# Loading a gate matrix and two expert matrices through GpSimd's DMA queue instead of ScalarE's

## The chip, the cores and the metric

The kernel runs on one core of one Trainium2 chip. The metric is the device time of one launch, in microseconds (us). A core has five engines that work from instruction queues of their own: TensorE (PE in the profile, with its weight loads shown apart as PEld), VectorE (DVE), ScalarE (ACT), GpSimd (POOL) and SyncE (SP). Sixteen DMA engines move data between the chip's main memory and the core's SBUF. A DMA is issued by an instruction in the queue of SP, ACT or Pool, and its landing is a semaphore that reaches 16.

## The reference, cut to what matters

Two stages are fused. The first is a linear recurrence along the sequence, for 8 batches of 6400 steps with 128 channels. The second treats all 51200 results as rows `x` of a mixture of low-rank adapters with 8 experts of rank 16, of which the two with the largest gate logits are used.

```
h = a[:, t] * h + b[:, t];  x[:, t] = h                 # 8 x 6400 x 128, float32
logits = x @ w_gate                                     # w_gate: 128 x 8
w = softmax over the two largest logits of a row
out = x + sum over the two experts e of  w_e * ((x @ A[e]) @ B[e])   # A: 8 x 128 x 16, B: 8 x 16 x 128
```

## The kernel before

The 51200 rows are cut into 100 units of 512 rows. A unit `w` goes through these steps, whose names are used below:

- `lda`, `ldb`: SP loads `a` and `b` (L632). Most loads bring two units (512 KB); four bring one (256 KB). The ring in SBUF holds 8 such loads of each, and a load waits until the unit that used its place 8 loads earlier has been transposed.
- `A`, `AB`: PE transposes `a` and `b` into PSUM with the identity `ident_f` (L632 to L677, recorded at L98). `aev`: ACT copies the transposed `a` to SBUF (L686). `scan`: DVE runs the recurrence (L710).
- `ZL`: PE multiplies the scanned block by `cst_h[:, 0:136]`, which holds the gate weights beside all of A (L749, recorded at L94). `zl`: ACT copies the result out (L767).
- gating (L781 to L907): DVE, Pool and ACT find the two largest logits and make the weights, for groups of one to three units.
- `mul`, `T`, `tev`, `D`, `oev`: weights times `x @ A` (Pool or DVE, L926), PE transposes, ACT or DVE copies back (L942), PE adds `x` and the product with B (L962, recorded at L94), ACT copies the sum to `outt` (L978). `st`: SP stores it, two units at a time, in an order that holds each store back by some 20 units (L995).

Every step is an operation of a planner (`_Plan`, L101). Each has a cost, a due key, a list of engines and a list of operations that it needs. `schedule` simulates all engines with one DMA link, starting at 700 ns, and always takes the operation that could start first, and of several that start together the one with the lowest key; a constant's key is its small negative number alone, so -110 goes ahead of -108. The order that comes out is written into each engine's queue, and the chip then works each queue strictly in that order with semaphore waits. A change of an operation's engine or number can so change the order of everything behind it.

The constants are set up at the head. Pool clears `ident_f` (`id0`, L435) and puts ones on its diagonal (`id`, L442). DVE makes `high`, `pick`, `mine` and the 16-bit copy `idh` from it (L490 to L524, L577). Three DMAs bring the weights to the tile `cst_f`: `wg_in` the gate weights (4 KB, 32 bytes for each of 128 partitions), `A_in` and `B_in` the expert arrays (64 KB each, 512 bytes a partition). Behind them:

- `spr0` on Pool and `spr1` on DVE (L533) spread A by expert, as soon as `A_in` and `mine` are done; `selA` (L542, eight matmuls on PE) gathers it, and `cstA` (L560, ACT) writes it to `cst_h`.
- `cstg` and `cstB` (L588, both on Pool) cast the gate weights and B to 16 bits, after `wg_in` and `B_in`.
- The first `ZL` needs `cstg` and `cstA`; the first `D` needs `cstB`.
- `table` (L480) is an activation on ACT that loads its table early.

All DMAs are recorded at L429, in `add_dma`.

Of the kernel before, what the change touches and what calls it, by code (L numbers as in the profile page):

```python
# [100 lines left out]
class _Plan:  # L101
# [15 lines left out]
    def add(self, name, eng, kind, unit, busy, emit, deps=(), dma=None, mode=None, takes=(), gives=None):  # L117
        self.ops[name] = _Op(name, eng, kind, unit, busy, self.latency, emit, list(deps), dma, mode, takes, gives)
# [161 lines left out]
def bass_associative_scan_2x2__then__mixture_of_adapters_kernel(  # L280
# [9 lines left out]
    E = moe_w_gate.shape[1]  # L290
# [78 lines left out]
    with ExitStack() as stack:  # L369
# [4 lines left out]
        cst_f = sb(nc.sbuf_tensor("cst_f", [128, E + 256], F32))  # L374
# [45 lines left out]
        def add_dma(name, eng, unit, starts, slot, ns, deps=(), kind="dma", issue=450.0, after=2000.0):  # L420

            if slot not in dma_sem:
                dma_sem[slot] = [sb(nc.semaphore("q_" + "_".join(map(str, slot)))), 0]
            dma_sem[slot][1] += 16 * len(starts)
            sem, value = dma_sem[slot]

            def emit(h):
                for dst, src in starts:
                    last = h.dma_start(dst, src).then_inc(sem, 16)  # L429
                return last  # L430

            add(name, eng, kind, unit, issue * len(starts), emit, deps, (sem, value, ns, after))
# [18 lines left out]
            ["id0"],  # L451
        )

        add_dma("wg_in", "act", -110, [(cst_f[:, 0:E], moe_w_gate[:, :])], ("wg",), 80.0, (), "fix", 450.0, 2000.0)
        add_dma(
            "A_in",
            "act",
            -109,
            [(cst_f[:, E : E + 128], moe_A.rearrange("e (h l) r -> (e h) (l r)", l=8))],
            ("A",),  # L460
# [5 lines left out]
        )  # L466
        add_dma(
            "B_in",
            "act",
            -108,  # L470
            [(cst_f[:, E + 128 : E + 256], moe_B.rearrange("e r d -> (e r) d"))],
            ("B",),
# [617 lines left out]
```

## Time and profile before

| what | value |
|---|---|
| median of 5 runs | 201.36 us (201.22 to 201.92) |
| the profiled execution's own time | 201.92 us |
| its span in the profile | 200.1 us |
| PE, ACT, DVE, POOL busy | 181.2, 179.5, 173.7, 158.4 us |
| moved by DMA | 79.30 MB, 396 GB/s over the span |
| read from main memory, written to it | 52.56 MB, 26.21 MB |
| granted TensorE clock, mean | 0.988 |

The profile page gives busy time by engine, then the span in 40 slices of 5 us with one digit (tenths) for each engine and the rate of all DMAs in GB/s. Section 3 of the page gives each DMA queue: its number, packets, MB, and the time that its packets took as a share of sixteen engines' span. Queue q1 is SP's, q10 is ACT's; q8 and q14 fetch instructions. In a timeline each row has the start, the length, the engine (a trailing q means its sequencer, which issues DMAs), the line, the operation and the tiles; brackets give the idle time ahead of it and what ended that. In a table of windows the DMA column is the mean busy share of the 16 DMA engines, and may pass 1 where packets of two queues overlap.

### The profile page before, as it was taken

How to read it: one execution, taken by the hardware profiler on the slowest of the kernel's cores; microseconds unless marked ns; L12 is line 12 of the kernel's file. 1: busy time of each engine (PE TensorE's matmuls, PEld its weight loads, DVE VectorE, ACT ScalarE, POOL GpSimd, SP SyncE). 2: the span in 40 equal slices, each digit the busy share in tenths (PEclk: the TensorE clock that was granted, in tenths of full speed). 3: DMA queues.
4: the chain of work that ended last, by engine and by line, in shares of the span. 5: the costliest groups of instructions: out<-in, count | busy, mean ns of one | idle time of the engine just before them, and what ended most of it. 6: DMA issues, size and time to landing. Idle time of an engine off the chain costs nothing.

```text
span 200.1 us, 8009 instructions
## 1 busy us (share of the span) xinstructions
PE 181.2 (91%) x3202; PEld 161.5 (81%) x3202; DVE 173.7 (87%) x302; ACT 179.5 (90%) x463; POOL 158.4 (79%) x278
## 2 busy tenths in 40 slices
PE   7687899999999999999999999999999999897640
PEld 4476788899999989899889998889898998795530
DVE  3599899999999998999989898799797998989910
ACT  3487999999999999999999999999999999898740
POOL 2243749989898999988699999998999988888700
PEclk9999999999999999999999999999999999999995
DMA  6999999999999999999999999999999999999991
GB/s 206 374 422 401 409 409 403 409 407 406 406 416 418 414 414 417 414 414 414 416 417 410 416 417 414 414 419 416 414 417 414 411 418 416 411 379 391 415 389 64
DMA packets 22629, 79.30 MB, mean 396 GB/s; under 512 B 2624, under 2 KB 2880, under 8 KB 22592
## 3 DMA queue, kind: packets, MB, share of 16 engines
q1 hardware_dynamic: 22160, 78.65, 97.8%
q8 instruction: 25, 0.41, 0.8%
q10 hardware_dynamic: 432, 0.14, 0.3%
q14 instruction: 12, 0.10, 0.1%
HBM read 52.56 MB, written 26.21 MB: 394 GB/s over the span
## 4 chain that ended last, share of the span: by engine, by line
PE 49%; DVE 15%; ACT 13%; DMA 12%; issue 3%; POOL 2%; SPq 2%; POOLq 1%; DVEq 0%; ACTq 0%
PE ps L94 25%; PE ps L98 24%; DMA a_in<-in_a_dram 12%; DVE xT L710 11%; ACT outt L978 4%; ACT a_st L686 4%; ACT zl L767 3%; DVE zwT L942 2%; SPq L429 2%; POOL zw L926 2%; POOLq L369 1%; ACT pn L816 1%; DVE zw L926 1%; POOL d L880 1%; ACT g L905 0%
## 5 line engine op out<-in xcount | busy, mean ns | idle before, releaser
L710 DVE TENSOR_TENSOR_SCAN xT<-a_st,xT,ps 128x512 f16<-128x512 f32 x96 | 120.2, 1252 | 10.5 <-PE ps L98 4.1
L926 POOL TENSOR_TENSOR zw<-zl,g 128x512 f16<-128x512 f32 x93 | 99.1, 1070 | 8.6 <-ACT g L905 6.5
L767 ACT COPY zl<-ps 128x408 f32<-128x408 f32 (+1 forms) x139 | 73.6, 536 | 0.9 <-PE ps L94 0.9
L98 PE MATMUL ps<-ident_f,a_in 64*128 64x64 f32 (+1 forms) x792 | 68.6, 229 | 2.3 <-DMA a_in<-in_a_dram 2.3
L98 PE MATMUL ps<-ident_f,b_in 64*128 64x64 f32 (+1 forms) x792 | 67.0, 229 | 1.8 <-DVE m L851 1.0
L686 ACT COPY a_st<-ps 128x512 f32<-128x512 f32 x100 | 61.5, 634 | 6.7 <-PE ps L98 6.0
L98 PEld LDWEIGHTS ps<-ident_f,a_in 64*128 64x128 f32 (+1 forms) x792 | 56.9, 139 | 9.7 <-DMA a_in<-in_a_dram 3.2
L978 ACT COPY outt<-ps 128x512 f32<-128x512 f32 x100 | 61.3, 628 | 2.1 <-PE ps L94 1.3
L98 PEld LDWEIGHTS ps<-ident_f,b_in 64*128 64x128 f32 (+1 forms) x792 | 55.9, 139 | 3.0 <-DVE m L851 1.1
L94 PE MATMUL ps<-cst_h,xT 128*128 128x136 f16 x400 | 50.3, 234 | 0.7 <-DVE xT L710 0.5
L94 PE MATMUL ps<-ident_h,xT 128*128 128x128 f16 x400 | 42.4, 229 | 1.4 <-DVE zwT L942 1.0
L98 PE MATMUL ps<-ident_h,zw 128*128 128x128 f16 x400 | 39.1, 220 | 3.7 <-DVE zw L926 2.0
L94 PEld LDWEIGHTS ps<-cst_h,xT 128*128 128x128 f16 x400 | 36.0, 148 | 4.5 <-DVE xT L710 1.3
L94 PE MATMUL ps<-cst_h,zwT 128*128 128x128 f16 x400 | 38.7, 219 | 0.0
L942 DVE COPY zwT<-ps 128x256 f32<-128x256 f32 x89 | 35.6, 408 | 2.6 <-PE ps L98 2.5
L94 PEld LDWEIGHTS ps<-ident_h,xT 128*128 128x128 f16 x400 | 32.9, 147 | 3.4 <-DVE zwT L942 2.3
L98 PEld LDWEIGHTS ps<-ident_h,zw 128*128 128x128 f16 x400 | 24.9, 97 | 7.7 <-DVE zw L926 3.0
L94 PEld LDWEIGHTS ps<-cst_h,zwT 128*128 128x128 f16 x400 | 27.1, 99 | 0.0
L816 ACT ACTIVATE pn<-d 128x96 f32<-128x96 f32 (+2 forms) x72 | 23.1, 329 | 0.8 <-POOL d L858 0.6
L866 POOL TENSOR_TENSOR L<-zl,pn 128x96 f32<-128x96 f32 (+2 forms) x34 | 12.8, 378 | 6.6 <-ACT pn L816 6.3
L888 POOL TENSOR_TENSOR d<-d 128x96 f32<-128x96 f32 (+2 forms) x36 | 13.8, 382 | 3.8 <-DVE d L841 3.3
L895 POOL TENSOR_TENSOR um<-d,pn 128x96 f32<-128x96 f32 (+2 forms) x36 | 14.2, 393 | 2.7 <-ACT pn L816 1.3
(38 smaller groups left out, 86.7 us busy)
## 6 DMA issues: line engine op xcount, KB each, us to landing
a_in<-in_a_dram SPq DMA_DIRECT2D x49, 512.0 KB, 15.5
b_in<-in_b_dram SPq DMA_DIRECT2D x49, 512.0 KB, 15.5
out_dram<-outt SPq DMA_DIRECT2D x49, 512.0 KB, 15.5
a_in<-in_a_dram SPq DMA_DIRECT2D x2, 256.0 KB, 8.9
b_in<-in_b_dram SPq DMA_DIRECT2D x2, 256.0 KB, 4.3
out_dram<-outt SPq DMA_DIRECT2D x2, 256.0 KB, 6.8
cst_f<-in_moe_A_dram ACTq DMA_DIRECT2D x1, 64.0 KB, 3.4
cst_f<-in_moe_B_dram ACTq DMA_DIRECT2D x1, 64.0 KB, 5.3
```

Source lines behind the costliest of these rows:

```text
L94: return self.handle.matmul(*args, **kwargs)
L98: return self.handle.transpose(*args, **kwargs)
L686: lambda h: h.copy(a_st[w % NAS][:, :], bank(("a", w))[:, :]),
L710: last = h.tensor_tensor_scan(out=x_at(lo, hi), data0=a_st[w % NAS][:, lo:hi], data1=bank(("b", w))[:, lo:hi], initial=init, op0=ALU.mult, ...
L767: return h.copy(zl[:, r0 : r0 + n, :], src)
L816: lambda h: h.activation(v(pn[s]), v(src[s]), ACTF.Relu, bias=bias, scale=scale),
L866: lambda h: h.tensor_tensor(out=v(L2[s]), in0=Lg, in1=v(pn[s]), op=ALU.subtract),
L888: lambda h: h.tensor_tensor(out=v(d1[s]), in0=v(d1[s]), in1=v(d2[s]), op=ALU.add),
L895: lambda h: h.tensor_tensor(out=v(um[s]), in0=v(d1[s]), in1=v(pn[s]), op=ALU.subtract),
L926: lambda h: h.tensor_tensor(out=oview, in0=zview, in1=gview, op=ALU.mult),
L942: return copy(zwT[v % NZT][:, :].bitcast(F32), bank(("O", v))[:, 0 : UT // 2])
L978: return copy(outt[:, v % NOUT, :], bank(("O", v))[:, :])
```

## The change

The three loads of the weights are issued by Pool (GpSimd's queue, in which software writes the descriptors) instead of ACT. The gate weights' number goes from -110 to -107, so among the three they come last instead of first. Nothing else is edited: the same bytes go to the same places, and the same operations wait for them.

```diff
-        add_dma("wg_in", "act", -110, [(cst_f[:, 0:E], moe_w_gate[:, :])], ("wg",), 80.0, (), "fix", 450.0, 2000.0)
+        add_dma("wg_in", "pool", -107, [(cst_f[:, 0:E], moe_w_gate[:, :])], ("wg",), 80.0, (), "fix", 450.0, 2000.0)
         add_dma(
             "A_in",
-            "act",
+            "pool",
             -109,
             [(cst_f[:, E : E + 128], moe_A.rearrange("e (h l) r -> (e h) (l r)", l=8))],
             ("A",),
...
         add_dma(
             "B_in",
-            "act",
+            "pool",
             -108,
             [(cst_f[:, E + 128 : E + 256], moe_B.rearrange("e r d -> (e r) d"))],
             ("B",),
```

## The prediction

> **What bounds the kernel now.** I read the page first: the rate of the DMAs by slices of 5 us, and the queues.
>
> ```profile
> GB/s 206 374 422 401 409 409 403 409 407 406 406 416 418 414 414 417 414 414 414 416 417 410 416 417 414 414 419 416 414 417 414 411 418 416 411 379 391 415 389 64
> q1 hardware_dynamic: 22160, 78.65, 97.8%
> q10 hardware_dynamic: 432, 0.14, 0.3%
> ```
>
> From slice 3 on the rate is flat at 400 to 420 GB/s, and SP's queue alone fills 97.8% of sixteen engines' span. ACT's queue, the one that the change empties, fills 0.3%, which is 0.003 x 200.1 = 0.6 us of each DMA engine. Next I read SP's timeline.
>
> ```profile
> 8.48 0.44 SPq L429 DMA_DIRECT2D a_in<-in_a_dram  x1
> 55.77 1.05 SPq L429 DMA_DIRECT2D a_in<-in_a_dram  x1
> 161.80 31.45 SPq L429 DMA_DIRECT2D out_dram<-outt  x19
> ```
>
> An issue takes 0.44 us while there is room and about 1.05 us later, one straight after the other: SP is held by the DMA engines, whose 512 KB take 512 KB / 413 GB/s = 1.27 us. After 161.8 us only 19 stores remain, and compute ends with a copy at 192.2 us. Is that copy the bound? The windows of the last microseconds and the time to landing of the last store (issued at 192.85 us) answer that; beside it stands the first load, of the same 256 KB, which went into empty queues.
>
> ```profile
> 194.00:195.00 1.00, 0.00 (x0) 0.00 (x0) 0.00 (x0) 0.00 (x0) 0.00 (x0) 1.00 1.00 399
> 195.00:196.00 1.00, 0.00 (x0) 0.00 (x0) 0.00 (x0) 0.00 (x0) 0.00 (x0) 0.73 0.59 227
> 197.00:198.00 1.00, 0.00 (x0) 0.00 (x0) 0.00 (x0) 0.00 (x0) 0.00 (x0) 0.50 0.09 37
> 198.00:199.00 1.00, 0.00 (x0) 0.00 (x0) 0.00 (x0) 0.00 (x0) 0.00 (x0) 0.50 0.06 25
> ```
>
> The columns after the stretch are its length, the busy time of PE, PEld, DVE, ACT and POOL, the granted clock, the DMA share and GB/s. Then the two landing times, the last store's first:
>
> ```profile
> DMA to landing us min/median/max: 6.8/6.8/6.8
> DMA to landing us min/median/max: 2.7/2.7/2.7
> ```
>
> The last store lands 6.8 us after its issue where an empty queue needs 2.7. A share of 0.06 is 0.06 x 16 = one DMA engine: the end is the one engine that is still behind while fifteen are done. For the store ahead (issued at 191.54 us, landing also 6.8 us later, with 256 KB in between, 0.6 us) the queue's part is 6.8 - 2.7 - 0.6 = 3.5 us. So compute could end about 3.5 to 4.1 us later and the last byte would still leave at the same time. I call this the cover. The chain of waits shows PE lines instead from 29 us on, because it follows semaphores, not a DMA engine's backlog.
>
> **The change part by part.** The start of the timeline before has every step that moves.
>
> ```profile
> 0.73 0.41 ACTq L429 DMA_DIRECT2D cst_f<-in_moe_w_gate_dram  x1
> 1.17 0.45 ACTq L429 DMA_DIRECT2D cst_f<-in_moe_A_dram  x1
> 1.65 0.45 ACTq L429 DMA_DIRECT2D cst_f<-in_moe_B_dram  x1
> 3.64 0.19 POOL L588 CAST cst_h<-cst_f 128x8 f16<-128x8 f32 x1 [2.18 <-DMA cst_f<-in_moe_w_gate_dram]
> 4.72 1.48 POOL L533 TENSOR_TENSOR spread<-cst_f,mine 128x384 f16<-128x384 f32 x1 [0.90 <-DMA cst_f<-in_moe_A_dram]
> 7.04 0.29 POOL L588 CAST cst_h<-cst_f 128x128 f16<-128x128 f32 x1 [0.84 <-DMA cst_f<-in_moe_B_dram]
> 8.46 0.31 PE L94 MATMUL ps<-cst_h,xT 128*128 128x136 f16 x2
> ```
>
> *ACT.* Three issues of 0.41 + 0.45 + 0.45 = 1.3 us go. ACT's table load then runs earlier, but its next work, the copy at 4.67 us, waits for PE's transposes of the first load. Gain: nothing.
>
> *Pool's order, worked by hand from the planner's rules.* Pool starts with `id0`; at 900 ns `id` is not yet ready, so `A_in` goes, then `id`, `B_in`, `wg_in`. Its planned landings become 5110 (A), 7310 (B) and 7580 (gate) instead of 5880, 7390 and 4470 ns. So `spr0` comes first among the users, then `cstB`, then `cstg`; and `selA`, ready earlier in the plan, probably goes ahead of unit 1's transposes on PE. Pool's queue behind the three issues is `spr0`, which waits for A anyway.
>
> *Price of an issue on Pool.* No row shows one. From below: ACT's 0.45 us. From above: Pool's costliest row here, `spr0`, 1.48 us. I take 1.0, nearer neither, and keep both ends. Then `A_in` is issued from 0.93 to 1.9 us, `id` is done at 2.3, `B_in` ends at 3.3 and `wg_in` at 4.3 us. (Ends: 1.4 and 2.4 for A; 2.6 and 5.7 for the gate.)
>
> *Late constants.* A landed 3.0 us after its issue ended (1.62 to about 4.6): now 4.9 us (4.4 to 5.4), so `spr0` ends at about 6.5 instead of 6.2. The gate weights took 2.4 us when queues were empty; B, issued into full ones, took 7.0 - 2.1 = 4.9. Issued third they resemble B: 4.3 + 4.9 = 9.2 us (from 2.6 + 2.4 = 5.0 to 5.7 + 4.9 = 10.6). With the cast `ZL` starts at about 9.5 instead of 8.46: about 1.0 us late (0 to 2.5). Behind it on PE's queue wait the transposes of later units, then the scans; `D` needs `cstB` only after 13 us. This lateness is covered twice: from 9 to 29 us PE still waits for loads (the chain there is 24 us of DMA of `a_in`), and at the end by the 3.5 us. Ring places come back late too, but loads were landing up to 15.5 us after issue, so the DMA engines have that much queued. On the path: 0. If the cover were gone it would cost its 1.0 us (at most 2.5).
>
> *`ident_f`.* `id` ends at 2.3 instead of 1.46 us; its first user on PE starts at 3.52, on the first load's landing. Cost 0; at 1.48 us an issue `id` is at 2.8, still covered.
>
> *The DMA engines themselves.* This is the only part on the path. The bytes are the same, on the same sixteen engines. Rates in the windows from 2 to 7 us are 250, 370, 343, 334 and 301 GB/s, against 410 after: (2050 - 1598) / 410 = 1.1 us lost while the queues fill and ACT's small packets pass between SP's. Most I can gain is that 1.1 us, if it is all due to the early small packets and they later pass for nothing; most I can lose is another 0.6 us, if the packets of a software queue take twice as long. A shift in time alone gives neither: the packets must still pass through engines that are full. I take 0.
>
> The page *DMA: Bandwidth & Descriptors* of the Trainium skill, section *SWDGE vs HWDGE vs iDMA*, calls hardware descriptor generation the faster setup, and its *Specifications* give about 1 us to the first byte for GpSimd's path against 0.6: by that each load would land some 0.4 us later, an estimate. *SBUF — State Buffer*, section *SBUF: two separate sides*, speaks against the change more strongly: while VectorE runs certain copies, GpSimd cannot write descriptors. No run shows it yet; by that rule the constants could slip by as much as VectorE's early work, and as long as this stays under the cover the sum is unchanged.
>
> *Sum.* Path terms: 0 (ACT) + 0 (lateness, 1.0 under a cover of 3.5) + 0 (DMA, -1.1 to +0.6). The profiled execution is its span of 200.1 and 1.8 around it, 201.92, the highest of five runs; the same change against the median 201.36 gives 201.4 us.
>
> **The rivals.**
>
> *Slower: the lateness outgrows the cover.* One mechanism: constants arrive late, or the new order lets compute's tail slip, until the last copy ends after 192.8 + 3.5 = 196.3 us. It decides when compute is more than 3.5 us late, and each us beyond costs one: 6 us late gives 201.4 + 2.5 = 203.9, 4.5 gives 202.4. For it: PE, ACT and DVE are 98%, 98% and 93% busy from 29 to 178 us (146.26, 146.19, 138.74 of 149), so nothing is made up there, and the planner's order changes from 1 us on. Against: the bounds above reach 2.5.
>
> *Faster: the start is freed.* The first loads no longer share the engines with 432 small packets, and the 1.1 us comes back in part: 200.3 to 200.8. For it: the low rates stand just where q10's packets pass. Against: they must pass at some time, and 0.6 of the 1.1 us is their own time.
>
> *It does nothing at the queue level.* If a Pool issue is as cheap as ACT's, all lands as before and the time is 201.4: the same number as mine.
>
> **How the numbers follow.** A measurement of this kernel can tell about 0.3% (0.6 us) from no change, so the middle is 200.8 to 202.0. My forecast with the last rival: 0.42. Slower: 0.34, for the untested order behind the change and a price of an issue that no row shows. Faster: 0.24. The range from 200.4 to 203.2 takes in most of the faster case and the slower one up to 1.8 us beyond the cover; it leaves out about 0.08 below and 0.12 above. The middle case alone would be 200.9 to 201.9.
>
> **What would show it.** Right: SP's 19 stores still end with a last landing some 6 us after issue; `spr0` ends near 6.5 us and the first `ZL` starts near 9.5; the Pool issues are 1 us apart; windows from 2 to 7 us hold about 1.6 MB. Wrong: the last store lands in about 2.7 us (compute became the bound), or the windows from 2 to 7 us carry much more (the start was freed), or a gap in Pool's rows longer than 1.5 us for an issue.

## The result and the profile after

The changed kernel took 202.5 us (median of 40 runs, 201.25 to 203.74), the kernel before beside it 201.57 us (77 runs). The ratio is 1.0041 with a 95% interval of 1.0032 to 1.0051, so the change costs about 0.0041 x 201.57 = 0.83 us. By the bound that the prediction set itself (0.3%, 0.6 us) that is slower, not the same. The profiled execution took 202.36 us, 0.44 more than the one of before, with a span of 200.6 us.

The page of after first: the rates by slices of 5 us, and the two queues.

```profile
GB/s 185 360 417 408 409 410 403 410 400 411 407 416 414 416 414 416 413 413 419 413 416 410 417 415 416 418 413 417 417 417 413 413 418 413 413 365 316 406 335 213
q1 hardware_dynamic: 22160, 78.65, 97.7%
q0 software_dynamic: 96, 0.14, 0.3%
```

SP's queue still fills its 97.7%: the bound is where it was. The same 0.14 MB now go in 96 packets instead of 432, and take the same share, 0.3%. The first two slices are lower (185 and 360 against 206 and 374), so are the four ahead of the last (365, 316, 406 and 335 against 379, 391, 415 and 389), where stores wait for late compute, and the last holds 213 against 64.

The start of the timeline of after:

```profile
1.30 0.70 POOL L429 DMA_DIRECT2D cst_f<-in_moe_A_dram  x1 [0.36 <-POOL ident_f L435]
2.34 0.56 POOL L429 DMA_DIRECT2D cst_f<-in_moe_B_dram  x1
2.90 0.71 POOL L429 DMA_DIRECT2D cst_f<-in_moe_w_gate_dram  x1
6.23 1.47 POOL L533 TENSOR_TENSOR spread<-cst_f,mine 128x384 f16<-128x384 f32 x1 [2.62 <-DMA cst_f<-in_moe_A_dram]
10.05 0.19 POOL L588 CAST cst_h<-cst_f 128x8 f16<-128x8 f32 x1 [1.26 <-DMA cst_f<-in_moe_w_gate_dram]
10.30 0.42 PE L94 MATMUL ps<-cst_h,xT 128*128 128x136 f16 x2 [0.59 <-POOL cst_h L588]
```

An issue on Pool takes 0.56 to 0.71 us, `id` (0.3 us) stands between the first two, and the last one ends at 3.6 us; on ACT all three had ended by 2.1. A landed at about 6.1, B at 8.4 and the gate weights at 10.0 us; they had landed at 4.6, 7.0 and 3.6. The first `ZL` starts 1.84 us later, at 10.30.

At the other end, the last output copies on ACT, the landing time of the last store, and two windows (columns as in the prediction):

```profile
193.99 1.57 ACT L978 COPY outt<-ps 128x512 f32<-128x512 f32 x3 [0.33 <-PE ps L94]
```

```profile
DMA to landing us min/median/max: 4.5/4.5/4.5
```

```profile
195.00:196.00 1.00, 0.00 (x0) 0.00 (x0) 0.00 (x0) 0.56 (x2) 0.00 (x0) 1.00 0.68 274
198.00:199.00 1.00, 0.00 (x0) 0.00 (x0) 0.00 (x0) 0.00 (x0) 0.00 (x0) 1.00 0.23 88
```

Compute ends at 193.99 + 1.57 = 195.56 us, 2.7 us later than before (192.82). Its last store lands 4.5 us after its issue. With 2.7 us for an empty queue, 1.8 us of that is still backlog: compute has used up part of the cover, not all of it, and yet the end is later. The prediction's two signs were some 6 us (right) and about 2.7 (wrong); 4.5 lies between them.

### The profile page after: what moved, and what is told of

The parts are those of the page before. It is cut to its first block, busy times and chain, and to the rows that moved or that the text cites. A ratio compares the mean times of both kernels' runs of the same rounds, so it can differ in the third digit from the quotient of the medians.

```text
span 200.6 us, 8030 instructions
## 1 busy us (share of the span) xinstructions
PE 183.8 (92%) x3202; PEld 164.2 (82%) x3202; DVE 173.9 (87%) x302; ACT 179.3 (89%) x461; POOL 160.6 (80%) x283
## 3 DMA queue, kind: packets, MB, share of 16 engines
q1 hardware_dynamic: 22160, 78.65, 97.7%
## 4 chain that ended last, share of the span: by engine, by line
PE 46%; DVE 22%; ACT 19%; issue 4%; DMA 4%; POOL 3%; ACTq 0%; DVEq 0%; POOLq 0%
PE ps L98 24%; PE ps L94 22%; DVE xT L710 18%; ACT a_st L686 7%; ACT outt L978 5%; ACT zl L767 4%; DMA cst_f<-in_moe_w_gate_dram 4%; DVE zwT L942 3%; ACT pn L816 2%; POOL zw L926 1%; ACT g L905 1%; ACT zwT L942 1%; POOL cst_f L429 1%; DVE m L851 0%; POOL d L858 0%
## 5 line engine op out<-in xcount | busy, mean ns | idle before, releaser
L767 ACT COPY zl<-ps 128x408 f32<-128x408 f32 (+1 forms) x139 | 71.9, 525 | 1.5 <-PE ps L94 1.5
L686 ACT COPY a_st<-ps 128x512 f32<-128x512 f32 x100 | 60.3, 618 | 6.8 <-PE ps L98 5.4
L978 ACT COPY outt<-ps 128x512 f32<-128x512 f32 x99 | 60.4, 617 | 1.7 <-PE ps L94 1.2
L98 PEld LDWEIGHTS ps<-ident_f,b_in 64*128 64x128 f32 (+1 forms) x792 | 56.7, 141 | 0.4
L94 PE MATMUL ps<-ident_h,xT 128*128 128x128 f16 x400 | 43.0, 231 | 1.0 <-DVE zwT L942 0.6
L942 DVE COPY zwT<-ps 128x256 f32<-128x256 f32 x90 | 36.3, 409 | 3.7 <-PE ps L98 3.7
L816 ACT ACTIVATE pn<-d 128x96 f32<-128x96 f32 (+2 forms) x72 | 21.9, 314 | 0.4 <-POOL d L858 0.3
L895 POOL TENSOR_TENSOR um<-d,pn 128x96 f32<-128x96 f32 (+2 forms) x37 | 13.6, 368 | 4.3 <-ACT pn L816 2.7
```

What stands on the lines that cost most here:

```text
L94: return self.handle.matmul(*args, **kwargs)
L98: return self.handle.transpose(*args, **kwargs)
L686: lambda h: h.copy(a_st[w % NAS][:, :], bank(("a", w))[:, :]),
L767: return h.copy(zl[:, r0 : r0 + n, :], src)
L816: lambda h: h.activation(v(pn[s]), v(src[s]), ACTF.Relu, bias=bias, scale=scale),
L895: lambda h: h.tensor_tensor(out=v(um[s]), in0=v(d1[s]), in1=v(pn[s]), op=ALU.subtract),
```

## The experiments

Four explanations stood against each other; the letters are those of the expectations below. **Order** (theory O): the planner's new order makes the late start of compute count. **Lateness** (L): the constants come late, and compute with them, whatever the order. **Queue** (Q): Pool's software queue holds up the DMA engines. **Time of issue** (T): small packets that are issued when the DMA engines are already full of SP's loads cost time that they do not cost at the very start, whichever engine issues them. "Compute ended" is the end of the last output copy in the profile; it was 192.82 us before.

### Order alone, and queue alone

The first kernel keeps after's order on every engine, but ACT issues the loads, at the head of its queue. Within the planner, behind its simulation:

```diff
+        loads = [ops[n] for n in ("wg_in", "A_in", "B_in")]
+        self.order["pool"] = [op for op in self.order["pool"] if op not in loads]
+        self.order["act"] = loads + self.order["act"]
+        for op in loads:
+            op.eng = "act"
```

> The changed kernel's order in every queue, but the three loads issued by ACT as before. Theory Q (the loads' passage through Pool's queue holds up some DMA engines in the first 10 us, and the last DMA engine sets the end): within 0.3 us of the kernel before, about 201.6. Theory O (the new order and the later start of compute use up the cover at the end): about 202.5, as the changed kernel, and the last store lands under 5 us after its issue.

It took 201.36 us against 201.49: ratio 0.9996 (0.9976 to 1.0016). Compute ended at 193.6.

The second keeps before's order on PE, ACT, DVE and SP, and gives the loads to Pool in after's sequence.

```diff
+        loads = [ops[n] for n in ("A_in", "B_in", "wg_in")]
+        self.order["act"] = [op for op in self.order["act"] if op not in loads]
+        head = [ops[n] for n in ("id0", "A_in", "id", "B_in", "wg_in", "spr0", "cstB", "cstg")]
+        self.order["pool"] = head + [op for op in self.order["pool"] if op not in head]
+        for op in loads:
+            op.eng = "pool"
```

> The order of the kernel before on PE, ACT, DVE and SP, with the three loads on Pool as in the changed kernel (Pool's own head in the changed kernel's order). Theory Q: about 202.5, and two DMA engines land the first 512 KB load about 2 us after the others. Theory O: the order's part is gone, about 201.6; what is left of it is the constants' lateness, at most 0.3 us.

It took 202.49 us: ratio 1.0045 (1.0027 to 1.0063). Compute ended at 195.51, and the last store landed 4.8 us after its issue. The forecast of two late DMA engines came half true: by the landing events of the trace, one of the sixteen parts of the first 512 KB load came 1.5 us behind the rest (8.2 us against 6.7). It says little, for two parts came 1.2 us behind (7.8 and 7.9 against 6.6) in the kernel with four idle copies below, which lost nothing. So the new order costs nothing, and the whole loss comes with the move of the three loads. Whether through their lateness, the queue or the time of issue is not told apart yet.

### Lateness without the loads

How late may compute be? Before's kernel, with `n` idle copies of a finished PSUM block on ACT ahead of unit 90's output copy:

```diff
+                for n in range(4 if v == 90 else 0):      # 10 in the second kernel
+                    copy(late_t[:, n, :], bank(("O", v))[:, :])
                 return copy(outt[:, v % NOUT, :], bank(("O", v))[:, :])
```

> The kernel before with four extra copies of one finished block (into a tile that nobody reads) on ACT ahead of unit 90's output copy, some 2.2 us: everything behind them on ACT ends later by up to that. If compute has a cover of 3.5 us at the end, as predicted: within 0.3 us of before. If the cover is not there: about 2 us slower.

> The same with ten copies, some 5.5 us. With a cover of 3.5 us: about 2 us slower than before, and the last store lands about 2.7 us after its issue. Without a cover: 5 us slower. If the DMA engines had more to spare than the landing times say: under 1 us slower.

With 4 copies compute ended at 196.08 (3.3 us late) and the time was 0.9998 of before (0.9983 to 1.0013). With 10 it ended at 198.70 (5.9 late) and the time was 1.005 (1.003 to 1.0069), 1.0 us. The landing time of the last store, with 4 copies and then with 10:

```profile
DMA to landing us min/median/max: 3.4/3.4/3.4
```

```profile
DMA to landing us min/median/max: 2.7/2.7/2.7
```

In the second the backlog is gone and compute is the bound; 2.7 us is the same as for the first load into empty queues. So the cover is real. Its size is best taken within the two profiles: the last store landed at 198.73 + 2.7 = 201.4 us, where before it was 192.85 + 6.8 = 199.65, so 5.9 us of lateness cost 1.8 and the cover is 4.1 us. The median's 1.0 us must not be set against this 5.9, since the profiled execution (203.72 us) was the slowest of the twelve.

The same lateness from the head: before's kernel with 16 more idle matmuls on PE at the start, the constants left early.

```diff
-                for _ in range(CFG["filler"][w]):
+                for _ in range(CFG["filler"][w] + (16 if w == 0 else 0)):
```

> The kernel before with 16 more filler matmuls on PE before unit 1 (some 3.5 us): compute starts as late as in the changed kernel, or later, with all loads where they were. Theory L (the changed kernel loses by its late constants, because compute runs about 2.7 us late to its end): 0.7 to 1 us slower than before. Theory Q (Pool's queue holds up DMA engines, lateness itself is covered): within 0.3 us of before.

It took 201.92 us against 201.64: 1.0007 (0.9993 to 1.0021). Compute ended at 195.57, within 0.01 us of after's 195.56. The landing time of the last store:

```profile
DMA to landing us min/median/max: 3.8/3.8/3.8
```

That pair is the sharpest reading of the study: the same end of compute, but 4.5 us to landing in after and 3.8 here. In these two profiles the DMA engines of after are 0.7 us further behind, and the two ratios differ by (1.0041 - 1.0007) x 201.6 = 0.7 us. The kernel with before's order and the loads on Pool (compute's end at 195.51, landing in 4.8 us, 1.0045) says the same. Compute that ends 2.7 us late, from the head on, costs at most 0.0021 x 201.6 = 0.4 us. The dip of the DMA rate near the end is no cost either: here it is deeper (355, 249, 403 and 381 GB/s in the same four slices).

### The packets without the lateness

Before's kernel, whose own loads stay as they are, loads the same three arrays a second time into a tile that nobody reads: on Pool at the places where after has its issues, and on ACT behind its three loads.

```diff
+        def extra(h, which):
...
+            h.dma_start(extra_t[:, lo:hi], src).then_inc(extra_sem, 16)
...
+        def table(h):                       # ACT; on Pool: A ahead of id, then B and g
+            for which in "ABg":
+                extra(h, which)
+            return h.activation(warm[:, :], warm[:, :], ACTF.Sigmoid)
```

> The kernel before with the same three arrays loaded a second time, into a tile that nobody reads, by Pool. Order and constants stay. Theory Q: the extra packets (0.6 us of each DMA engine) plus the hold-up: 0.8 to 1.5 us over before. Theory O: nothing waits for them, so no more than the 0.6 us that the extra packets take.

> The control to the second load by Pool: the same second load by ACT. Both theories: the extra packets alone, 0.2 to 0.6 us over before. Theory Q puts it 0.5 to 1 us under the second load by Pool, theory O puts the two level.

Pool's second set cost 1.0055 (1.0036 to 1.0074), 1.1 us; compute ended at 194.38. ACT's cost 1.0041 (1.0026 to 1.0056), 0.83 us; compute ended at 193.14, only 0.3 us late. ACT's issues in the timeline of the latter:

```profile
2.14 0.44 ACTq L445 DMA_DIRECT2D extra_t<-in_moe_A_dram  x1
2.62 0.45 ACTq L445 DMA_DIRECT2D extra_t<-in_moe_B_dram  x1
3.10 0.49 ACTq L445 DMA_DIRECT2D extra_t<-in_moe_w_gate_dram  x1
```

By its bytes the set is worth 0.14 MB / 410 GB/s = 0.34 us. Issued between 2.1 and 3.5 us it cost 0.83 us (0.52 to 1.13) on a hardware queue as well. Adding a late set costs about what after pays for moving its only set late, and Pool's set no more than ACT's beyond the noise. But the added packets' own share of the engines, 0.6 us by the prediction's reading, lies inside that interval, so these two runs show no price on top of it.

### Only the time of issue

Here ACT keeps the loads, and only their time changes. First they stand behind ACT's table activation, in the order A, B, gate:

```diff
+        loads = [ops[n] for n in ("A_in", "B_in", "wg_in")]
+        self.order["act"] = [ops["table"]] + loads + [op for op in self.order["act"] if op not in loads + [ops["table"]]]
+        head = [ops[n] for n in ("id0", "id", "spr0", "cstB", "cstg")]
+        self.order["pool"] = head + [op for op in self.order["pool"] if op not in head]
```

> The order of the kernel before, the three loads by ACT, but in Pool's order (A, B, gate) and behind ACT's table load, so that they are issued at about 2.2, 2.7 and 3.2 us; Pool's users in the order A, B, gate. Theory Q: within 0.3 us of before, since ACT's queue does not hold engines up. Theory L: slower by as much of 0.9 us as the constants are late here. A third theory, T (small packets that pass once the engines are full cost time whatever the queue): 0.5 to 0.9 us slower.

As a test of lateness it failed: ACT loaded its table from 0.73 to 2.01 us, and the issues went out beside that, at 0.91, 1.32 and 1.79 us. It took 201.5 us against 201.64, 1.0001 (0.9985 to 1.0017), and so shows only that the order A, B, gate is free, with the gate weights issued 1.1 us later than before.

In the next one A also waits for DVE's `pick`:

```diff
         loads = [ops[n] for n in ("A_in", "B_in", "wg_in")]
+        loads[0].deps.append(ops["pick"])
```

> As the run with the three loads behind ACT's table load (order of the kernel before, loads by ACT in the order A, B, gate), but the first of them now waits for DVE's pick tile, so that they are issued at about 2.6, 3.1 and 3.5 us and their packets pass at about 4 to 8 us, when the DMA engines are full, as in the changed kernel. Theory T (late small packets cost, whatever the queue): 0.5 to 0.9 us slower than before. Theory Q (it is Pool's queue): within 0.3 us of before.

Its timeline on ACT's queue:

```profile
2.60 0.39 ACTq L434 DMA_DIRECT2D cst_f<-in_moe_A_dram  x1
3.02 0.45 ACTq L434 DMA_DIRECT2D cst_f<-in_moe_B_dram  x1
3.49 0.69 ACTq L434 DMA_DIRECT2D cst_f<-in_moe_w_gate_dram  x1
```

It took 202.93 us against 201.59: 1.0052 (1.003 to 1.0073). The loads landed at 8.3, 10.6 and 12.0 us. Compute ended 4.3 us late, which is the whole cover of 4.1. Yet of the stores issued from 183 us on none landed in less than 3.3 us, and the last took 4.0, not 2.7: the DMA engine that finishes last was never without work, and so still set the end. The hardware queue, issued late, costs as much as Pool's. This run alone does not part time of issue from lateness, because no filler was run that makes compute as late as 4.3 us.

The counterpart is a Pool load issued early: A alone goes to Pool, ahead of `id`; B and the gate weights stay on ACT.

```diff
+        load = ops["A_in"]
+        self.order["act"] = [op for op in self.order["act"] if op is not load]
+        head = [ops["id0"], load]
+        self.order["pool"] = head + [op for op in self.order["pool"] if op not in head]
+        load.eng = "pool"
```

> The kernel before with A alone on Pool (issued after the identity's clearing), B and the gate weights on ACT as before. Theory Q with a price for each load: about 0.3 us slower. Theory Q with the hold-up on the first load alone, while the queues fill: 0.7 to 0.9 us slower.

```profile
1.28 0.70 POOL L434 DMA_DIRECT2D cst_f<-in_moe_A_dram  x1 [0.34 <-POOL ident_f L440]
```

That row of its timeline shows the same start and price as after's first issue. The time was 201.62 us against 201.59, 1.0005 (0.9978 to 1.0031), and A landed 4.0 us after its issue against 4.8 in after. After's A is issued no later than this one; of its three loads it is B and the gate weights, 68 KB, that are late, by 0.7 and 2.2 us.

### The queues in the steady state

Last, eight extra loads of B (64 KB each) spread over the run, issued by Pool (with `mul`) in one kernel and by ACT (with `aev`) in the other:

```diff
+                if v % 10 == 5 and v < 80:      # Pool; on ACT the eight units w = 15, 25, ..., 85
+                    extra(h, v // 10)
```

> The kernel before with eight extra 64 KB loads of B by Pool, spread over the run ahead of the products of units 5, 15, ... 75, into a tile that nobody reads. Their 0.5 MB are 1.3 us of all DMA engines. If each load through Pool's queue holds up the slowest DMA engine by some 0.3 us more than one through ACT's: 2 us over the control and about 3.5 us over before. If the hold-up belongs to the first microseconds alone: level with the control.

> The control: eight extra 64 KB loads of B by ACT, spread over the run ahead of the copies of units 15, 25, ... 85. All theories: 1.3 to 1.6 us over before, the time of the packets on the slowest DMA engine; ACT's 8 x 0.45 = 3.6 us of issues stay about under the cover.

Pool's took 1.0081 (1.0052 to 1.011), ACT's 1.0088 (1.0053 to 1.0123). The queue lines, Pool's kernel and then ACT's (whose 432 first packets are the constants):

```profile
q0 software_dynamic: 256, 0.52, 0.7%
```

```profile
q10 hardware_dynamic: 1584, 0.66, 1.2%
```

The two queues cost the same: 1.6 and 1.8 us for 0.52 MB, which by bytes are 0.52 / 410 = 1.3 us. The Trainium skill, *DMA: Bandwidth & Descriptors*, section *Issuing engines are not separate DMA queues*, says that DMAs of all issuing engines run on the same sixteen engines, and that starting them from several engines at once saves only the sequencer's time of starting them. These two kernels agree.

## Why the prediction was right or wrong

- **Bound and cover: right.** DMA engines set the end, and late compute is free up to a point. The prediction worked out 3.5 to 4.1 us; the idle copies gave 4.1.
- **Price of an issue on Pool: too high.** 0.56 to 0.71 us where 1.0 was taken; the bounds held. Pool's three issues stand in series with its own wait (0.36 us) and `id`, so they still began at 1.30, 2.34 and 2.90 us.
- **Landings: later than said for A.** A landed at 6.1 us, beyond the upper end of 5.4: it needed 4.1 us after its issue ended, not 3.0. Fifteen of its sixteen parts had landed by 5.0 us, and the last came 1.1 us behind them. With A alone on Pool, issued at the same time, it was 3.3 us; what held that one part up in after is not shown. The gate weights' 10.0 and `ZL`'s 10.30 (9.2 and 9.5 taken) lie inside their bounds. The lockout of GpSimd's descriptor writing (the Trainium skill, *SBUF — State Buffer*, section *SBUF: two separate sides*) left no large mark: the issue from 2.90 to 3.61 us, beside two casts on DVE at 2.91 and 3.05, took 0.71 us against 0.70 for the first. Whether these casts are among the copies that lock GpSimd out, no run here shows.
- **Lateness on the path: right at 0, its size too small.** About 1.0 us was worked out, at most 2.5. `ZL` started 1.84 us late and compute ended 2.7 us late, the half clock of the last section included. The head filler with the same end cost nothing that can be measured.
- **The step that failed: the DMA engines' term of 0.** "A shift in time alone gives neither: the packets must still pass through engines that are full." The shift alone costs 1.0041 on Pool, 1.0045 with before's order, and 1.0052 on ACT's own queue: 0.8 to 1.0 us, more than the 0.6 us allowed for a dearer software queue. That bound was also tied to the wrong property: equal bytes on the two queues cost the same. Moving the set later was taken as neutral, with no row that shows it.
- **The rivals.** "Slower" gave 202.4 for 4.5 us of lateness, near the 202.5 measured, but by a mechanism that did not happen. "Faster" fell: the windows from 2 to 7 us carried 1.50 MB instead of 1.60, less, not more. "Nothing at the queue level" was right about the queue, as far as the pairs tell, and wrong about the time of issue. The range held 202.5, but by its allowance for lateness beyond the cover, which is luck; the likeliest case, 200.9 to 201.9, did not hold it.

What is shown: kernels whose small loads had all started to be issued by 1.8 us lie between 0.9996 and 1.0007 (order alone, head filler, A behind the table, A on Pool). Kernels with such loads started between 2.1 and 3.5 us lie between 1.0041 and 1.0055, on either queue, with compute 0.3 to 4.3 us late. That after's loss is due to the time of issue follows by exclusion: order (the first kernel), lateness of this size (the head filler) and queue (the pairs on Pool and ACT) are each shown to cost nothing that can be measured. No single run changes the time of issue and nothing else.

What fits but is not shown: that the early set passes almost free while the queues are still filling, and that a late one displaces SP's loads. (The engines are not idle there: from 2 to 7 us their mean share in before is 0.99.) That the late set costs the same whether moved or added speaks for it, but the early loads' own cost would be seen only in a kernel without them, and none was run. Nor do the first microseconds of single profiles settle it: with before's head untouched, the windows from 2 to 7 us averaged 320 GB/s in the kernel before and 299 and 307 in those with idle copies at the tail, which lost nothing there, so after's 300 proves nothing. And what the price is made of is open: 0.34 us by bytes lies below every interval, 0.6 by the packets' share of the engines (0.003 x 200 us) lies inside that of ACT's second set (0.52 to 1.13) and just under that of after (0.65 to 1.03, from 0.0032 to 0.0051 of 201.57), where only B and the gate weights are late.

## What to carry to other kernels

In a kernel that its DMA engines bound, as here, issue small constant loads at the very start; here the loss went with a delay of 0.7 us (B) and 2.2 us (gate weights) in issuing them, and not with the queue or with compute's lateness. To know whether late work matters, compare the last store's landing time with that of a load into empty queues (6.8 and 2.7 us here), then confirm the difference with dummy work at the tail (4.1 us here). Late compute under that cover is free, but the same delay may move a transfer, and that is priced separately.

## What was not expected of the hardware

A slower granted TensorE clock: the median over the runs is 0.98 in after, 0.988 in the kernel before beside the idle copies. Two windows of the same stretch, before and then after (the clock is the number ahead of the DMA share):

```profile
7.00:12.00 5.00, 4.71 (x78) 3.79 (x77) 3.15 (x9) 3.56 (x10) 0.92 (x4) 1.00 1.02 414
```

```profile
7.00:12.00 5.00, 3.56 (x25) 2.77 (x25) 1.43 (x3) 1.41 (x4) 1.18 (x3) 0.61 1.02 399
```

In after PE waits for `spread` from 5.69 to 7.85 us, and the clock is 0.5 from 8.1 to 14.9 us. So 1.8 us at the first `ZL` became 3.0 at the second unit's scan (11.70 instead of 8.69). The Trainium skill, *TensorE: Matmul & The Clock Gate*, section *What's actually happening*, gives an idle window of about 3.4 us ahead of a half clock; here 2.2 us without a matmul preceded it. It is part of the lateness under the cover. The change is not needed for it: with before's head, the profiles of the four idle copies, the ten idle copies and Pool's eight extra loads show a pause of PE of 1.6, 1.7 and 2.6 us there, on a late load, and then 3.4 us at a clock of 0.5 (from 9.3, 8.0 and 8.2 us). In the kernel before the pause was 1.3 us, and the clock stayed at 1.
